# One kernel, one change: the first product of three blocks by 49 small products instead of 7 larger ones

## The chip, the cores and the metric

The kernel runs on one core of a Trainium2 chip. The core has five engines that run at the same time, each working through its own list of instructions in order: TensorE (PE, matrix products, with its weight loads shown as PEld), VectorE (DVE), ScalarE (ACT), GpSimd (POOL) and SyncE (SP), which here does nothing but issue DMAs. Data lies in HBM; on-chip memory of 128 partitions (SBUF) feeds the engines; TensorE writes into PSUM. The metric is the time of one execution in microseconds (us), the median of several runs.

## The reference

```python
# attention: q, k, v of shape (4, 8, 768, 64); gamma differs by head
for t in range(S):
    state = gamma * state + einsum('bhd,bhe->bhde', k[:, :, t], v[:, :, t])
    y[:, :, t] = scale * einsum('bhd,bhde->bhe', q[:, :, t], state)
x = y.transpose(0, 2, 1, 3).reshape(3072, 512)
h = x @ w_in                            # 512 -> 2048
g = h * (1 / (1 + exp(-1.702 * h)))
out = g @ w_out                         # 2048 -> 512
```

All of it is in float32 (the weights arrive as float64 and are narrowed in the kernel).

## The kernel before, in words

**Tiling.** The 3072 tokens are worked in `NB` = 6 blocks of 512, each of four attention chunks (a chunk is 64 tokens of two batch rows). A block's x lies transposed in the tile `X` as four quarters: two halves of the 512 features by two halves of the 512 tokens, each quarter two feature rows of 128 by 256 tokens. `X` has seven places, so that sums of quarters fit as well. `G` holds the gated hidden layer of one block, `W2` the weights of the second product, `W1A` and `W1B` those of the first (`W1B` in the two tiles tagged `late`, whose space is lent in between to `ring` and `own` of the second product, so that `W1B` is stored once and loaded again in each later block).

**Stages.** Block 0 uses plain products (`up0`), block 1 a form written out by hand (`seven`), blocks 2 to 5 `up(d)` for d = 0 to 3 (L555 to L597). A call of `up` computes a quarter of the hidden layer by the seven-product scheme: a 2 x 2 block product made of seven products of sums of quarters instead of eight. Each of the seven is four TensorE instructions of 128x128 weights against 256 columns (L562). ACT copies three partial results out of PSUM (L569, L576, L583), DVE adds PSUM and copy (L572, L580, L586, L588), ACT gates (L393), DVE forms sums for what follows (L594 to L597).

The second product of blocks 2 to 5 is `down49(m)`: two levels of the scheme, 49 products, each four instructions of 128 columns (L666), in 14 units (i, half), i from 0 to 6. Its inner weight sums were formed by `inner_w2` and lie in HBM (`W2D`); `stream` brings them back (POOL queue, L635), `derive` forms the sums of `G` (DVE, L655 to L657).

**Attention** is laid between units. After units 1, 4, 7 and 10 of `down49` of blocks 2 to 4 comes `step(j, j-1)`: PE computes `pa` and `py` (L289 to L312), DVE masks and adds, POOL scales k (`kd`, L274) and the state (L359). `step` reads q and k of its chunk transposed, which `turn(j)` does (DVE, L253). At its end, `turn(j)` issues the 16 loads of q and k for chunk j + 2 (SP, L157); `step(j)` issues four loads of k and four of v for chunk j + 1 (SP, L143). In `up` of block m, `turn` of the chunk that the first `step` of `down49(m)` needs stands after d = 0.

**Order.** On PE all instructions run as written. On the other engines a scheduler orders them, except those passed through `pin` or `keep_in_program_order`, which stay as written. SP's list is one: a DMA that waits holds all that are behind it.

Of the kernel before, what the change touches and what calls it, by code (L numbers as in the profile page):

```python
# [9 lines left out]
F32 = mybir.dt.float32  # L10
U32 = mybir.dt.uint32
AF = mybir.ActivationFunctionType
ALU = mybir.AluOpType
P = 128
# [14 lines left out]
def kernel(  # L29
# [59 lines left out]

    W1A = const.tile([P, NP // 2, 7, 2, P], F32, name="W1A")  # L90
    W1B = [late.tile([P, 2, 7, 2, P], F32, name=f"W1B{i}", tag=f"late{i}") for i in range(2)]
    W1D = [dram.tile([P, 2, 7, 2, P], F32, name=f"W1D{i}") for i in range(2)]
    W2D = [dram.tile([P, 3, NP // 2, P], F32, name=f"W2D{i}") for i in range(7)]
# [12 lines left out]
    whole_h = const.tile([P, H], F32, name="whole_h")  # L106
    ident = const.tile([P, P], F32, name="ident")
    mask = const.tile([P, 2, HP, D], F32, name="mask")
    state = [const.tile([P, 2, HP, D], F32, name=f"state{i}") for i in range(2)]


    def w1(p):

        return (W1A, p) if p < NP // 2 else (W1B[p // 2 - 2], p % 2)

# [66 lines left out]
    class Narrow:  # L182
# [4 lines left out]
        def __init__(self, i):  # L187
            n, p, h = (1 if i < 2 else 2), i // 2 % NP, i % 2

            if i < 2:  # L190
                m = W1A[:, 1, 2 * h:2 * h + 2].rearrange("p s c f -> p (s c f)")
                w = W1A[:, 0, h:4:2].rearrange("p ab c f -> p c ab f")
            elif i < NFF:
                t, q1 = w1(p)
                m = t[:, q1, 0:4].rearrange("p s c f -> p (s c f)")
                w = t[:, q1, 0:4].rearrange("p (ab h) c f -> p (h c) ab f", ab=2)
            else:
                m = w = W2[:, 0:4, p]
            x = raw(i, n).rearrange("p (n two) -> p n two", two=2)
            self.lo, self.hi, self.m, self.w, self.i = x[:, :, 0], x[:, :, 1], m, w, i  # L200
            if i >= NFF:
                self.lo, self.hi = [t.rearrange("p (s e) -> p s e", s=4) for t in (self.lo, self.hi)]
            self.mu = m.bitcast(U32)
# [191 lines left out]
    def g(m, p, s):  # L395

        if m:
            return G[:, p:p + 2, s, :]
        if s < 3:
            t, q1 = w1(p)  # L400
            return t[:, q1:q1 + 2, 4 + s].rearrange("p a c f -> p a (c f)")
        return X[:, 4 + p // 2] if p < 6 else G0
# [4 lines left out]
    def up0(th, p, tag):  # L407

        h = ps.tile([P, 2, TH], F32, name="ph", tag=tag)
        t, q1 = w1(p)  # L410
        for ab in range(2):
            for c in range(4):
                w = t[:, q1, 2 * ab + c // 2, c % 2, :]
                pe.matmul(h[:, ab], w, X[:, 2 * th + c // 2, c % 2, :], start=(ab == 0 and c == 0), stop=(c == 3),  # L414
                          skip_group_check=True)
        if th == 0:
            return t[:, q1, 4:6].rearrange("p s c f -> p (s c f)"), h
        return [(g1(0, p, 2 + i), i) for i in range(2)], h

    def up1(f):  # L420

        p, ab = divmod(f, 2)
        h = ps.tile([P, 2, TH], F32, name="ph", tag="xy"[f % 2])
        t, q1 = w1(p)
        for c in range(4):
            w = t[:, q1, 2 * ab + c // 2, c % 2, :]
            pe.matmul(h, w, X1[:, c // 2:4:2, c % 2, :], start=(c == 0), stop=(c == 3))
        return G[:, p, ab:4:2, :], h
# [12 lines left out]
    def seven_4(d):  # L441

        t, q1 = w1(2 * d)
        SUM_W[d] = m = [t[:, q1:q1 + 2, n].rearrange("p u c f -> p u (c f)") for n in range(4)]
        m.append(one.tile([P, 2, 2 * P], F32, name="w4", tag="qT", bufs=2))
        m.append(one.tile([P, 2, 2 * P], F32, name="w5", tag="at", bufs=2))
        m.append(two.tile([P, 2, 2 * P], F32, name="w6", tag="o"))
        pin(dve.tensor_add(m[4], m[2], m[3]))
# [72 lines left out]
    def sums_w1(p):  # L521
        t, q1 = w1(p)
        w = [t[:, q1:q1 + 2, s] for s in range(7)]
        pool.tensor_add(w[4], w[2], w[3])
        pool.tensor_sub(w[6], w[0], w[2])
        pool.tensor_sub(w[5], w[4], w[0])
        pool.tensor_sub(w[2], w[1], w[5])

    def sums_x():
        tc.keep_in_program_order(pool.tensor_sub(X[:, 4], X[:, 2], X[:, 0]))  # L530
        pool.tensor_sub(X[:, 6], X[:, 3], X[:, 2])
        pool.tensor_sub(X[:, 5], X[:, 3], X[:, 4])
        pool.tensor_sub(X[:, 2], X[:, 1], X[:, 5])

    def sums_w2(p):
# [19 lines left out]
    def up(d):  # L555

        t, q1 = w1(2 * d)

        def product(acc, sa, sb, start, stop):
            for u in range(2):  # L560
                for c in range(2):
                    pe.matmul(acc[:, u, :], t[:, q1 + u, sa, c, :], X[:, sb, c, :],  # L562
                              start=(start and u == 0 and c == 0), stop=(stop and c == 1), skip_group_check=True)
# [34 lines left out]


    ORDER = [(0, 0), (1, 2), (3, 5), (2, 6), (0, 4), (1, 3), (2, 1)]  # L600

# [29 lines left out]

    def stream(ring, i):

        c = ring[:, i % 2 * 3:i % 2 * 3 + 3]
        pool.dma_start(c, W2D[i])  # L635
        return c

    def begin_ring():

        ring = late.tile([P, 7, 4, P], F32, name="ring", tag="late0")  # L640
        return ring, {i: stream(ring, i) for i in range(2)}

    def down49(m, ring, comps):

        b, t0 = m * CB // NC * 2, m * CB % NC * D
        rows = out.rearrange("(b t) (e c) -> e t b c", b=B, c=EH)[:, t0:t0 + TH, b:b + 2, :] \
            .rearrange("e (h p) b c -> h e p b c", p=P)
        own = late.tile([P, 7, 4, P], F32, name="own", tag="late1")
        acc, kept = {}, {}

        def derive(i):
            q = [G[:, u::2, ORDER[i][0], h * P:(h + 1) * P] for u in range(2) for h in range(2)]
            a11, s3, a12, s2 = q
            d = own[:, i % 2 * 3:i % 2 * 3 + 3]
            dve.tensor_add(d[:, 0], s2, a11)  # L655
# [16 lines left out]

        flat = X[:, 4:6].rearrange("p s c t -> p (s c t)")
        def keep(name, half):
            if half == 0:
                if name in "pt":
                    home2(name, flat[:, 0:4 * P], flat[:, 4 * P:7 * P])
                else:
                    home2(name, (own if name == "u" else ring)[:, 6].rearrange("p j e -> p (j e)"),
                          one.tile([P, 2 * EH], F32, name=name, tag="s2" if name == "u" else "s3"))  # L680
            return kept[name][half]
# [16 lines left out]
        def then(i, half, p0):  # L698
            if i == 0:
                act.activation(keep("p", half), p0, AF.Copy)  # L700
            elif i == 1:
                put(0, 0, half, p0, "p")
            elif i == 2:
                act.activation(keep("u", half), p0, AF.Copy)
            elif i == 3:
                act.activation(keep("v", half), p0, AF.Copy)
            elif i == 4:
                u = kept["u"][half]
                dve.tensor_add(keep("t", half), p0, u)
                put(1, 1, half, p0, "v")  # L710
            elif i == 5:
                put(0, 1, half, p0, "t")
            else:
                put(1, 0, half, p0, "v")
# [21 lines left out]
        for i in range(7):  # L736
            for half in range(2):
                def unit(i=i, half=half):
                    if half == 0:
                        if i == 0:  # L740
                            pairs[0] = derive(0)
                        x = "x" if i in (0, 2, 3) else "y"
                        if i != 2 and i != 3:
                            for n in range(2):
                                acc[x, n] = ps.tile([P, 4 - n, P], F32, name="pq", tag=x)
                    x = "x" if i in (0, 2, 3) else "y"
                    if i == 6 and half == 1 and m == NB - 1:
                        finish(acc[x, half], pairs[i][half])
                        return
                    products(acc[x, half], pairs[i][half], i not in (2, 3))  # L750
                    then(i, half, acc[x, half])
                    if half == 0 and i < 6:
                        pairs[i + 1] = derive(i + 1)
                    if half == 1:
                        if i + 2 < 7:
                            comps[i + 2] = stream(ring, i + 2)
                        if i in (0, 1, 3):
# [208 lines left out]
    for m in range(NB):  # L966
# [8 lines left out]
        elif 1 < m < NB - 1:  # L975
# [3 lines left out]
            if last == NCH - 1:  # L979
                between.append(lambda: step(None, NCH - 1))  # L980
        if m > 1:
            if m > 2:
                W1B[:] = [late.tile([P, 2, 7, 2, P], F32, name=f"W1B{i}", tag=f"late{i}") for i in range(2)]
                pool.dma_start(W1B[0], W1D[0])
            for d in range(NP // 2):
                up(d)
                if d == 0 and m > 2:
                    pool.dma_start(W1B[1], W1D[1])
                if d == 0 and m < NB - 1:
                    turn((m + 1) * CB + 1)  # L990
                if d == NP // 2 - 2:
                    ring = begin_ring()
                if m == 2 and d < 2:
                    tc.keep_in_program_order(sp.dma_start(W1D[d], W1B[d]))
                if m == 2:
                    for i in range(2 * d, min(7, 2 * d + 2)):
                        inner_w2_t3(i)
        for n, unit in enumerate(down(m) if m < 2 else down49(m, *ring)):
            unit()
# [8 lines left out]
            if between and (n in (2, 5, 11, 16, 21) if m == 1 else n % 3 == (1 if m else 2)):  # L1008
                between.pop(0)()
            if 0 < m < NB - 1 and n == (23 if m == 1 else 11):  # L1010
                sums_x()


# [44 lines left out]
```

## Time and profile before

| | |
|---|---|
| median of 3 runs | 662.12 us (660.49 to 664.74) |
| the profiled execution: span | 660.5 us (no other time is recorded for it; the fastest run is 660.49) |
| PE busy | 642.2 us, 97% |
| DVE, POOL, ACT busy | 453.9, 198.8, 159.0 us |
| stage `up` of blocks 2, 3, 4, 5 | from 261.5, 362.9, 464.7 and 564.8 us, each 48.35 us |
| `down49` of blocks 2, 3, 4, 5 | from 309.9, 411.2, 513.1 and 613.2 us |

The page of a profile gives busy times per engine, the span in 40 slices, the DMA queues, the chain of work that ended last, and groups of instructions. Times inside a line are start or sum in us and mean ns of one. One TensorE instruction in float32 is two records in the trace, so "x8" in a timeline is four instructions.

### The profile page before, as it was taken

Reading aid. Unit: us, or ns where it says so; the run is one execution under the profiler, and the core shown is the slowest. Engines: PE = TensorE matmul, PEld = TensorE weight load, DVE = VectorE, ACT = ScalarE, POOL = GpSimd, SP = SyncE. Lnnn points to the kernel's source line nnn. Section 1 sums busy time; section 2 is a strip of 40 time slices with the busy share of each in tenths; the row PEclk is TensorE's granted clock in tenths of the full one; section 3 lists DMA queues with packets and bytes.
Section 4 is the critical chain, followed back from the end, with each engine's and each line's share of the span. In section 5 each row is a group of like instructions: output and inputs, shape, how many; then the busy total and the mean of one; then the engine's idle time right before and its main releaser. Section 6 shows DMA issues by size and latency. Waiting matters only on the chain.

```text
span 660.5 us, 15291 instructions
## 1 busy us (share of the span) xinstructions
PE 642.2 (97%) x6390; PEld 580.2 (88%) x6390; DVE 453.9 (69%) x645; ACT 159.0 (24%) x306; POOL 198.8 (30%) x225
## 2 busy tenths in 40 slices
PE   6789999999999999999999999999999999999997
PEld 3778888888788888889999888999888999988997
DVE  3699989999936973556984445995354995254965
ACT  4674233551000000333100233010233110233110
POOL 6400311310379217000536400445600255500000
PEclk9989999999999999999999999999999999999999
DMA  9995549763233556262485832386742252602142
GB/s 176 193 274 173 152 104 241 172 163 60 49 82 135 137 149 153 58 248 96 118 199 134 279 57 97 86 223 135 225 118 97 66 154 104 235 21 96 55 154 96
DMA packets 148149, 91.86 MB, mean 139 GB/s; under 512 B 131600, under 2 KB 134416, under 8 KB 147056
## 3 DMA queue, kind: packets, MB, share of 16 engines
q1 hardware_dynamic: 135856, 45.19, 29.8%
q0 software_dynamic: 9888, 44.46, 20.6%
q10 hardware_dynamic: 2336, 1.25, 0.6%
q8 instruction: 50, 0.82, 0.5%
q14 instruction: 19, 0.16, 0.1%
HBM read 72.89 MB, written 15.47 MB: 134 GB/s over the span
## 4 chain that ended last, share of the span: by engine, by line
PE 89%; DVE 4%; DMA 4%; SPq 1%; issue 1%; ACT 0%; DVEq 0%
PE pq L666 27%; PE px L562 17%; PE pd L799 13%; PE py L562 13%; PE ph L491 7%; PE ph L414 5%; PE pa L289 2%; PE py L312 2%; PE pa L297 2%; PE py L306 2%; DMA W<-in_moe_w_in_dram 1%; DMA W<-in_moe_w_out_dram 1%; DMA q_in<-in_q_dram 1%; PE pt L250 1%; SPq L140 1%
## 5 line engine op out<-in xcount | busy, mean ns | idle before, releaser
L635 POOL DMA_DIRECT2D ring<-W2D x28 | 15.4, 551 | 227.7 <-PE px L562 118.3
L666 PE MATMUL pq<-W,G 128*128 128x128 f32 x672 | 80.2, 276 | 0.0
L666 PEld LDWEIGHTS pq<-W,G 128*128 128x128 f32 x672 | 77.6, 192 | 1.3 <-issue 0.7
L666 PE MATMUL pq<-ring,own 128*128 128x128 f32 x448 | 60.1, 276 | 1.3 <-issue 1.3
L562 PE MATMUL px<-X,W1A 128*128 128x256 f32 x256 | 59.8, 379 | 0.0
L562 PE MATMUL px<-X,W1B 128*128 128x256 f32 x256 | 59.8, 379 | 0.0
L666 PEld LDWEIGHTS pq<-ring,own 128*128 128x128 f32 x448 | 54.5, 192 | 0.4
L562 PEld LDWEIGHTS px<-X,W1B 128*128 128x128 f32 x256 | 48.5, 190 | 6.7
L562 PEld LDWEIGHTS px<-X,W1A 128*128 128x128 f32 x256 | 48.4, 190 | 6.5
L393 ACT ACTIVATE G<-G 128x512 f32<-128x512 f32 x60 | 37.4, 628 | 54.7 <-DVE G L572 33.4
L799 PE MATMUL pd<-W,G 128*128 128x256 f32 x224 | 49.6, 381 | 0.0
L799 PEld LDWEIGHTS pd<-W,G 128*128 128x128 f32 x224 | 42.2, 190 | 5.9
L562 PE MATMUL py<-X,W1A 128*128 128x256 f32 x192 | 45.4, 379 | 0.0
L562 PE MATMUL py<-X,W1B 128*128 128x256 f32 x192 | 45.4, 379 | 0.0
L562 PEld LDWEIGHTS py<-X,W1A 128*128 128x128 f32 x192 | 36.5, 190 | 5.0
L562 PEld LDWEIGHTS py<-X,W1B 128*128 128x128 f32 x192 | 36.5, 190 | 5.0
L580 DVE TENSOR_TENSOR t<-py,u 128x512 f32<-128x512 f32 x16 | 11.1, 692 | 32.3 <-PE py L562 32.3
L569 ACT ACTIVATE p<-px 128x512 f32<-128x512 f32 x16 | 9.6, 597 | 96.0 <-PE px L562 96.0
L414 PE MATMUL ph<-X,W1A 128*128 128x256 f32 x128 | 30.6, 397 | 0.9 <-DVE X L347 0.9
L594 DVE TENSOR_TENSOR G<-G 128x512 f32<-128x512 f32 (+2 forms) x24 | 12.3, 513 | 25.7 <-ACT G L393 25.7
L666 PE MATMUL pq<-ring,G 128*128 128x128 f32 x224 | 29.6, 275 | 0.0
L666 PE MATMUL pq<-W,own 128*128 128x128 f32 x224 | 29.6, 275 | 0.0
(237 smaller groups left out, 1226.0 us busy)
## 6 DMA issues: line engine op xcount, KB each, us to landing
ring<-W2D POOLq DMA_DIRECT2D x28, 768.0 KB, 4.8
W1B<-W1D POOLq DMA_DIRECT2D x6, 1792.0 KB, 9.8
W<-in_moe_w_in_dram SPq DMA_DIRECT2D x12, 512.0 KB, 5.9
W<-in_moe_w_out_dram SPq DMA_DIRECT2D x10, 512.0 KB, 5.8
out_dram<-o POOLq DMA_DIRECT2D x20, 256.0 KB, 3.0
q_sq<-in_q_dram SPq DMA_DIRECT2D x144, 32.0 KB, 2.1
k_sq<-in_k_dram SPq DMA_DIRECT2D x144, 32.0 KB, 2.1
v_in<-in_v_dram SPq DMA_DIRECT2D x72, 64.0 KB, 3.1
```

The costliest lines, as they stand in the source:

```text
L289: pe.matmul(pa[HALF[w], u, 0, s, :], kt[HALF[u], w, s, :], qt[HALF[u], w, s, :], start=True, stop=True)
L297: pe.matmul(pa[HALF[u], w, 1, s, :], kd[HALF[w], HP * u + s, :], vn[HALF[w], HP * u + s, :], start=True, stop=True)
L306: pe.matmul(py[HALF[o], u, 1, 2 * w + s2, :], old[HALF[u], w, 2 * s2 + o, :], qt[HALF[u], w, 2 * s2 + o, :], start=True, stop=True)
L312: pe.matmul(py[HALF[o], w, 0, 2 * u + s2 if f < NEW else 2 * s2 + u, :], vn[HALF[w], HP * u + s, :], a[HALF[w], u, s, :], start=True, stop ...
L393: pin(act.activation(g, h[:, i], AF.Gelu_apprx_sigmoid))
L414: pe.matmul(h[:, ab], w, X[:, 2 * th + c // 2, c % 2, :], start=(ab == 0 and c == 0), stop=(c == 3), skip_group_check=True)
L491: pe.matmul(acc[:, u, :], w, x, start=(start and u == 0 and c == 0), stop=(stop and c == 1), skip_group_check=True)
L562: pe.matmul(acc[:, u, :], t[:, q1 + u, sa, c, :], X[:, sb, c, :], start=(start and u == 0 and c == 0), stop=(stop and c == 1), skip_group_ ...
L594: dve.tensor_sub(q[0][1], q[0][0], q[0][1])
L635: pool.dma_start(c, W2D[i])
L666: pe.matmul(p0[:, j, :], a[:, d], w[:, d], start=(new and j == 0 and d == 0), stop=(d == NP // 2 - 1), skip_group_check=True)
L799: pe.matmul(p0[:, n, :], g1(m, p, sa)[:, n * P:(n + 1) * P], W2[:, sb, p, :], start=(new and p == 0 and n == 0), stop=(last and p == NP - ...
```

## The change

Blocks 3 to 5 compute the first product by `up49` in place of `up`. Each of the seven products is itself made of seven products of 128 x 128 x 128, so a block has 4 x 49 = 196 instructions of 128 columns in place of 112 of 256. The units (a product P1 to P7 of a pair d) are written in an order that interleaves the four pairs; the attention's PSUM buffers (`pa`, `py`) are used for the odd pairs. A unit has two halves, of four and three instructions. The seven inner results are combined by five adds for each quarter (`post`, on POOL or DVE as the table `then` says), before the gate.

The inner sums of x are formed in place and by `derive_x` (DVE); those of the weights once, in block 2 (`inner_w1`: DVE, POOL, stored to HBM as `T1D` and `Q1D` by SP), and come back in every block of 3 to 5 by 28 loads on SP (`fetch_t` of 192 or 384 KB, `fetch_q` of 256 KB). Five of them are issued after unit 11 of `down49` of the block before (`before_up49`), the others within `up49`. `w_in` is laid out as `W1A` (the four quarters) and `W1L`, a view of the tile `LATE` (the three sums); in blocks 3 to 5 `LATE` holds what is fetched, the sums of x, and the working space of `down49`. `turn` of the chunk that the first `step` of `down49` needs stands behind `up49` as a whole; the first two `stream`s of each of these blocks go to SP. In `down49` one kept partial result (`t`) goes, as its products are added in PSUM.

```diff
-    W1A = const.tile([P, NP // 2, 7, 2, P], F32, name="W1A")
-    W1B = [late.tile([P, 2, 7, 2, P], F32, name=f"W1B{i}", tag=f"late{i}") for i in range(2)]
-    W1D = [dram.tile([P, 2, 7, 2, P], F32, name=f"W1D{i}") for i in range(2)]
+    W1A = const.tile([P, NP, 4, 2, P], F32, name="W1A")
+    LATE = late.tile([P, 2 * NP * 3, P], F32, name="LATE")
+    W1L = LATE.rearrange("p (n s c) f -> p n s c f", s=3, c=2)
+    T1D = [dram.tile([P, 7, 3, P], F32, name=f"T1D{d}") for d in range(NP // 2)]
+    Q1D = [dram.tile([P, 2, 3, 2, P], F32, name=f"Q1D{d}") for d in range(NP // 2)]
...
+    def sums_x_inner():
+        lo, hi = [slice(i * P, (i + 1) * P) for i in range(2)]
+        x = X[:, 0:4]
+        pin(dve.tensor_sub(x[:, :, 0, hi], x[:, :, 0, lo], x[:, :, 0, hi]))
+        pin(dve.tensor_sub(x[:, :, 1, hi], x[:, :, 1, hi], x[:, :, 0, hi]))
+        sums_x()
+        derive_x(0)
...
+    def inner_w1(d):
+        b11, b12, b21, b22 = w1_quarters(d, 0)
+        t = []
+        for k, a in enumerate((b12, b22, b21)):
+            t.append(one.tile([P, 4, P], F32, name=f"w1t{k}", tag="at", bufs=2) if k != 1 else
+                     two.tile([P, 4, P], F32, name=f"w1t{k}", tag="tmp", bufs=1))
+            tc.keep_in_program_order(dve.tensor_sub(t[k], a, t[k - 1] if k else b11))
+            sp.dma_start(T1D[d][:, 0:4, k], t[k])
...
+    UNITS = [("P1", 0), ("P2", 0), ("P1", 1), ("P2", 1), ("P6", 0), ("P5", 0), ("P7", 0), ("P4", 0), ("P3", 0),
+             ("P6", 1), ("P5", 1), ("P7", 1), ("P1", 2), ("P4", 1), ("P2", 2), ("P3", 1), ("P6", 2), ("P5", 2),
+             ("P7", 2), ("P1", 3), ("P4", 2), ("P2", 3), ("P3", 2), ("P6", 3), ("P5", 3), ("P7", 3), ("P4", 3),
+             ("P3", 3)]
...
+    def fetch_t(d, s, slot):
+        n = 1 if s == 6 else 2
+        c = LATE[:, SLOT[slot]:SLOT[slot] + 3 * n].rearrange("p (s k) f -> p s k f", k=3)
+        pin(sp.dma_start(c, T1D[d][:, s:s + n]))
...
+    def before_up49():
+        fetch_t(0, 0, "C")
+        fetch_t(1, 0, "B")
+        for s in (5, 4, 6):
+            fetch_q(0, s)
...
+        def products(p0, prod, d, half):
...
+            pairs = [(a12, b21), (s2, t2), (s3, t3), (d0, t1)] if half == 0 else [(a11, b11), (d2, t4), (d1, b22)]
+            new = prod in ("P1", "P2", "P5")
+            for j in ((0, 2, 1, 3) if half == 0 else (0, 2, 1)):
+                a, b = pairs[j]
+                pe.matmul(p0[:, j, :], b, a, start=(new and j == 0), stop=True, skip_group_check=True)
...
+        def post(eng, d, s):
...
+            pin(eng.tensor_add(top, top, m1))
+            pin(eng.tensor_add(h1u0, h1u0, h0u1))
+            pin(eng.tensor_add(one_e(2), one_e(2), h1u1))
+            pin(eng.tensor_add(h1u1, h1u1, h1u0))
+            both = at(b + 1, d, [*K, [7 * P, 2]])
+            pin(eng.tensor_add(both, both, E[:, :, 1:3] if K else E[:, k, 1:3]))
...
+        A, B = (0, 3), (1, 2)
+        then = {
+            1: [lambda: derive_x(1), lambda: fetch_t(0, 2, "C")],
...
+            15: [lambda: fetch_t(2, 2, "C"), lambda: post(dve, 1, B), lambda: presum(0, B), lambda: outer(0)],
+            16: [lambda: fetch_q(3, 5), lambda: gate(1, A)],
+            17: [lambda: fetch_q(3, 4), lambda: fetch_t(3, 4, "B")],
+            18: [lambda: fetch_q(3, 6), lambda: fetch_t(3, 6, "S"), lambda: post(pool, 2, A), lambda: gate(1, B),
+                 lambda: presum(1, A)],
+            21: [lambda: post(dve, 3, (0,))],
+            22: [lambda: fetch_t(3, 2, "C"), first_stream, lambda: post(pool, 2, B), lambda: presum(1, B), lambda: outer(1)],
+            23: [lambda: gate(3, (0,)), lambda: gate(2, A)],
+            24: [lambda: presum(3, (0,)), lambda: presum(2, A)],
+            25: [lambda: post(dve, 3, (3,))],
+            26: [lambda: post(pool, 3, (1,)), lambda: gate(3, (3,)), lambda: gate(2, B)],
+            27: [lambda: post(dve, 3, (2,)), lambda: gate(3, (1,)), lambda: gate(3, (2,)), lambda: presum(2, B),
+                 lambda: outer(2), lambda: presum(3, (3,)), lambda: presum(3, (1,)), lambda: presum(3, (2,)),
+                 lambda: outer(3)],
+        }
...
+                if prod in ("P1", "P6", "P7"):
...
+                    pin(act.activation(kept[name][half], p0, AF.Copy))
+                elif prod == "P4":
+                    pin(act.activation(place(d, 1, half), out(p0, half), AF.Copy))
+            if prod == "P2":
+                add(d, 0, "p", "y")
+            elif prod == "P7":
+                add(d, 3, "v", "y")
+            elif prod == "P3":
+                add(d, 2, "u", "y")
...
-        if m > 1:
-            if m > 2:
-                W1B[:] = [late.tile([P, 2, 7, 2, P], F32, name=f"W1B{i}", tag=f"late{i}") for i in range(2)]
-                pool.dma_start(W1B[0], W1D[0])
...
+        elif m > 2:
+            comps = {}
+            ordered[0] = True
+            up49(first_stream=lambda: comps.update({0: stream(0, sp)}))
+            ordered[0] = False
+            if m < NB - 1:
+                turn((m + 1) * CB + 1)
+            comps[1] = stream(1, sp)
...
+            if 1 < m < NB - 1 and n == 11:
+                ordered[0] = True
+                sums_x_inner()
+                before_up49()
+                ordered[0] = False
```

## The prediction

> **What bounds the kernel now.** I read the page's busy times first, then the windows of each stage, then the chain of work that ended last.
>
> ```profile
> PE 642.2 (97%) x6390; PEld 580.2 (88%) x6390; DVE 453.9 (69%) x645; ACT 159.0 (24%) x306; POOL 198.8 (30%) x225
> ```
>
> ```profile
> 362.80:411.20 48.40, 48.40 (x227) 42.61 (x226) 21.90 (x34) 16.40 (x27) 9.52 (x13) 1.00 0.49 148
> 411.20:464.70 53.50, 52.85 (x906) 52.02 (x905) 42.65 (x64) 3.87 (x7) 25.84 (x29) 1.00 0.57 140
> ```
>
> The columns of the windows are length and sum, then PE, PEld, DVE, ACT, POOL, clock, DMA share, GB/s. PE works without a gap in block 3's `up` (48.4 us) and nearly so in its `down49`. So time goes only if PE has less to do, and comes back wherever PE must wait. DVE is idle for more than half of `up`, but for only a fifth of `down49`.
>
> **What PE saves.** The chain gives the rate of 128-column instructions:
>
> ```profile
> 411.22 6.25 PE pq L666 x56
> 613.16 43.78 PE pq L666 x392
> ```
>
> 392 records are 196 instructions: 0.2233 us each. A block's `up` is 112 instructions in 48.35 us, `up49` 196 in 43.8. Three blocks: 3 x 4.6 = **-13.9 us**, if PE never waits.
>
> **First wait: SP's list at the start of blocks 3 and 4.** The timeline of SP in block 2's `down49` and after (start, length, count):
>
> ```profile
> 319.95 3.48 SPq L143 DMA_DIRECT2D kn_in<-in_k_dram  x4
> ...
> 358.48 4.01 SPq L157 DMA_DIRECT2D q_sq<-in_q_dram  x8
> 362.60 3.90 SPq L157 DMA_DIRECT2D k_sq<-in_k_dram  x8
> 366.59 2.58 SPq L143 DMA_DIRECT2D kn_in<-in_k_dram  x4
> 369.27 2.79 SPq L143 DMA_DIRECT2D v_in<-in_v_dram  x4
> 379.14 5.95 SPq L157 DMA_DIRECT2D q_sq<-in_q_dram  x8
> ```
>
> From 319.95 to 372.06 SP issues 80 loads without a rest, 0.65 us each. Waits cannot explain it; SP's waits in that stretch are
>
> ```profile
> SPq L143 <- POOL kd L274: 32.3, 1, 32.3
> ...
> SPq L157 <- DVE qT L253: 0.5, 1, 0.5
> ```
>
> the first of which is the one before 319.95. So SP finishes this list 9.2 us after `up` of block 3 has begun (362.87). Today that is harmless. In the compiled order of the changed kernel the same 80 loads stand there, released by the same `kd`, and behind them the five fetches of `before_up49`. The first (384 KB) is issued at 372.1 and lands some 3.5 us later (an estimate between 256 KB stores, 3.0 us, and 768 KB `ring` loads, 4.8 us, in the page's DMA list). P1 of pair 0 needs it in its third instruction, at 363.3. **+12.5 us** (bounds 10 and 15). The later fetches follow at about 0.65 us, the units at 1.56, so they keep ahead.
>
> **Second wait: the transposes that moved.** `turn` stood after d = 0 of `up`; now it is behind `up49`, and on DVE behind its whole tail. From the last unit's release to the second transpose DVE has, by the rows for each width (512 elements 0.69, 384 0.55, 256 0.42, 128 0.29, 1024 1.21): rest of `add` and `derive(0)` 1.9, `post`, `add`, `post` 4.7, `presum` of pairs 2 and 3 and `outer` of both 5.3, `sums_g_outer` 1.2, `derive(1)` 2.1, transposes 1.4: 16.6 us, of which 1.6 lie under the last unit. PE comes to `step` after units 0 and 1, 28 instructions or 6.25 us. 15.0 - 6.25 = 8.8; independent DVE instructions start 0.60 apart instead of 0.69, which takes up to 2.2. I take 8 in blocks 3 and 4 (bounds 5 and 10): **+16**. Block 5 has no `step`, but its second product (slot 1) needs `presum` and `derive(1)` from the same tail: **+2** (0 to 4).
>
> **Third: SP again, block 4.** In block 3's `down49` the 16 loads that `turn` issues also move: they wait for the transposes, end of `up49` + 15 us, and 96 loads follow at 0.65 = 62.5, so the first fetch lands at 15 + 62.5 + 4 = 81.5. PE is there after 53.5 + 8 + 0.5 = 62. **+18.5** (at the fastest row, 8 in 4.00 us, only +5). In block 4 there are 28 loads, and the fetches are early: nothing.
>
> **Fourth: DVE and POOL within `up49`.** DVE had 21.9 us of work in `up`. Now: 12 `add` pairs of 1.24, `derive_x` 2.9, four `post` 7.8, `presum` 7.3, `outer` 5.5, `derive(0)` 2.1, 40 us in 43.8. POOL gets five `post` of pairs (2 x 1.27 + 3 x 0.75 = 4.8 each) and a single of 2.8, 27 us. Both read two SBUF inputs, and the trace shows what happens when they meet: `inner_w2`'s subtractions alone, then beside POOL's sums:
>
> ```profile
> 249.01 1.42 DVE L612 TENSOR_TENSOR X<-W,X 128x512 f32<-128x512 f32 x2
> 200.49 4.09 DVE L612 TENSOR_TENSOR X<-W,X 128x512 f32<-128x512 f32 x2
> ```
>
> ```profile
> 201.07 1.28 POOL L526 TENSOR_TENSOR W1A<-W1A 128x512 f32<-128x512 f32 x1
> ```
>
> 0.7 us becomes 2.0: one waits for the other. (Additions that read PSUM keep their 0.68 beside POOL.) The tight place is the end. From P3 of pair 1 (25.0 us into the stage) DVE is free at 26.4 and has 17.4 us of listed work until the `add` that frees P3 of pair 3's PSUM, due at 42.1: 1.7 late by its own work. Two POOL `post`s of pair 2 lie in the same stretch, 9.5 us; some 4 of them can hide under the `add`s from PSUM. 1.7 + 9.5 - 4 = 7.2; I take 7 in each block, **+21** (bounds 1 and 11 each).
>
> **Small terms.** Block 2: 16 DVE and 16 POOL instructions and 36 stores (`inner_w1`) beside a DVE that is half idle; the stores of one shared buffer follow each other through SP and reach into the last quarter: +0.5 (0 to 4). PE after a long wait: at 21.8 us of the trace, when PE had mostly waited, four transposes' eight records took twice their later time, and at 26 us still did:
>
> ```profile
> 21.81 1.11 PE L250 MATMUL pt<-ident,kn_in 128*128 128x128 f32 x4
> 31.65 0.60 PE L250 MATMUL pt<-ident,kn_in 128*128 128x128 f32 x4
> ```
>
> Before, PE never waits long after that; now four times by 8 us or more. PE was slow for 5.5 us without rest from 20.75, which loses up to 2.3 us. I take 1 for each: **+4** (0 to 9). [...]
>
> [...]
>
> **Sum.** -13.9 + 12.5 + 16 + 2 + 18.5 + 21 + 0.5 + 4 = +60.6 on the profiled span of 660.5: 721. The median of the runs lies 1.6 above that span: **723 us**.
>
> **Rivals.** (a) DVE and POOL don't hinder each other in `up49` (other tiles, other order of arrival): 21 becomes 3, **705**. For it: collisions in the trace don't always lengthen DVE. (b) SP gets through its list in time, as 32 KB loads may go faster than when DMAs of `W1B` and stores compete (their bytes are gone from the POOL queue): no first and third wait, two restarts fewer, 60.6 - 31 - 2 = 27.6, **690**. Against it: the waits listed above are too short to be the pace. (a) and (b) together **672**. (c) On the other side, faster: all loads, transposes and DVE's tail hide, and only PE counts: 660.5 - 13.9 + 1 for copies that end just late (P7 to P4) + 1.6: **649**. It decides if SP's fetches land before 363.3 and the transposes end within 6.25 us of `up49`. Only a different order of instructions than the compiled one would do it. (d) The products themselves don't run at 0.223, as each goes to another PSUM place instead of four in a row: at the 276 ns of one such matmul, +10.4 a block, of which 7 hide under DVE's lag: **733**.
>
> **Chances.** Forecast 0.56 (710 to 740), (a) 0.17, (b) 0.09, both 0.05, (c) 0.05, (d) 0.05; no change 0.03. The range of 8 in 10 runs from 685, near (b), to 745, which takes in (d) and the upper bounds of two terms. Faster by over 1% (about what this kernel's runs can tell from no change) 0.05, within 1% 0.03, slower 0.92.
>
> **What would show it.** Right: PE idle at the first unit of blocks 3 and 4, put to a DMA of `LATE`; PE `pa` waiting for DVE `qT` once in blocks 3 and 4; SP's list unbroken over both stage borders; block 5 the shortest of the three; DVE lines of `post` above 0.8 us for 256 elements. Wrong: SP idle before the fetches, or `up49` at 44 us in all blocks.

## The result, and the profile after

The changed kernel takes **755.7 us** (median of 4 runs, 754.1 to 758.7) against 663.4 us (660.5 to 665.0) of the kernel before on the same chip: 1.140 times as long, 95% interval 1.135 to 1.144. The forecast was 723, with a range of 685 to 745: the sign was right, the size 33 us short. The profiled execution has a span of 754.9 us, 94.4 more than before.

The page's line of busy times and its row of the granted clock:

```profile
PE 653.8 (87%) x6894; PEld 602.8 (80%) x6894; DVE 533.9 (71%) x794; ACT 182.1 (24%) x348; POOL 300.9 (40%) x319
...
PEclk9999999999999999999779998995999899999999
```

PE's share has fallen from 97% to 87%, and its clock now dips, which it never did before after the start. DVE has 80 us more to do, POOL 102. The windows of the first and second product of block 3, and of the first product of block 5 (length and sum, PE, PEld, DVE, ACT, POOL, clock, DMA share, GB/s):

```profile
364.57:444.64 80.07, 52.66 (x394) 50.63 (x393) 36.66 (x63) 21.98 (x38) 35.51 (x37) 0.85 0.48 138
444.64:505.90 61.26, 54.99 (x906) 53.96 (x905) 49.91 (x80) 5.99 (x10) 27.40 (x34) 0.94 0.58 142
...
644.79:707.50 62.71, 50.17 (x394) 47.91 (x393) 38.34 (x65) 22.08 (x38) 32.08 (x34) 0.95 0.42 130
```

Before, these were 48.40, 53.50 and 48.30 us. Even block 5, which has no late fetch and no late transposes, takes 14.4 us longer, and the clock falls to 0.85 in block 3. What PE waited for (total, times, longest):

```profile
PE pw L707 <- DMA LATE<-T1D: 31.2, 2, 15.7
PE pw L707 <- ACT u L819: 18.1, 6, 3.3
PE pa L295 <- DVE kT L259: 12.5, 2, 6.2
PE pw L707 <- ACT p L819: 6.2, 6, 1.2
PE pw L707 <- ACT v L819: 4.5, 6, 0.7
PE pw L707 <- ACT G L821: 4.2, 6, 0.8
```

The first and third line are the forecast's fetches and transposes. The others (34.9 us, with 1.9 for `v49b` further down) are waits for **ACT's copies out of PSUM**, for which the forecast's sum has nothing (its rival (c) allows 1 us for copies from P7 to P4). Those shown come 6 times each: twice a block, for pairs 1 and 3. Pairs 0 and 2 run the same code and have none. The difference is in `banks`: an even pair's accumulator is two PSUM tiles, one for each half of a unit; an odd pair's is one tile of 8 places, cut in two. In the compiled order PE's second half of an odd pair carries a wait for ACT's copy of the first half, although it writes other places.

The chain of work that ended last shows what stands before such a copy, in block 5, from DVE's `add` after P7 of pair 0 on (its short pieces named `issue` are left out):

```profile
659.17 0.47 DVE e L736
659.73 1.27 POOL G L754
661.07 0.73 POOL G L755
661.79 0.70 POOL e L756
662.56 0.73 POOL G L757
663.36 1.27 POOL G L759
664.65 0.04 ACT e L821
665.04 0.60 ACT u L819
665.68 5.04 PE pw L707 x28
```

POOL's `post` of pair 0 takes 4.9 us. The buffer `e49` has two places; P4's copy on ACT needs the one that this `post` is reading, so it waits; the copy of `u` stands behind it on ACT; and PE's second half of P6 stands behind that copy. In pair 3 the way is longer: DVE's add for P2 waits for POOL's `post` of pair 2, DVE's own `post` and the first add that reads `u` of pair 2 follow it, and only then may ACT write the next `u` (timeline):

```profile
692.29 0.56 DVE L736 TENSOR_TENSOR e<-pw,LATE 128x384 f32<-128x384 f32 x1 [1.08 <-POOL G L759]
...
695.34 0.60 ACT L819 ACTIVATE u<-pw 128x512 f32<-128x512 f32 x1 [5.90 <-DVE G L736]
```

What PE does after the wait for `u` of pair 1 (timeline; x2 is one instruction):

```profile
662.46 0.39 PE L707 MATMUL pw<-LATE 128*128 128x128 f32 x2
665.68 0.49 PE L707 MATMUL pw<-X,w1q 128*128 128x128 f32 x2 [2.84 <-ACT u L819]
666.01 0.39 PE L707 MATMUL pw<-LATE,w1q 128*128 128x128 f32 x2
...
667.17 0.63 PE L707 MATMUL pw<-X,LATE 128*128 128x128 f32 x2
...
670.09 0.39 PE L707 MATMUL pw<-X,LATE 128*128 128x128 f32 x2
```

From 666.5 to 670.1 instructions start 0.43 us apart instead of 0.22. Summed over the stretches in which they do, PE lost 9.5 us after the six waits for u, 5.2 after the two fetches and 3.5 after the two waits for kT: **18.2 us**.

With these, the span's 94.4 us add up:

| | forecast | measured |
|---|---|---|
| PE's saving | -13.9 | -13.7 |
| waits for fetches (terms 1 and 3) | 12.5 + 18.5 | 31.2 |
| transposes, block 5's tail (term 2) | 16 + 2 | 12.5 + 0 |
| waits within `up49` (term 4) | 21 | 35.3 |
| slow clock after waits | 4 | 18.2 |
| blocks 0 to 2 | 0.5 | 1.8 |
| ends of waits | none | 9.1 |

The last row is the remainder, and has a size of its own: idle time is counted from a record's end, 0.39 us after its start, where the next instruction would have started after 0.22, and the one after a wait lasts 0.1 longer. That is some 0.28 us for each of 32 waits, 9.0.

### The profile page after: what moved, and what is told of

It reads as the page before. It is cut to its first block, busy times and chain, and to the rows that moved or that the text cites. A ratio compares the mean times of both kernels' runs of the same rounds, so it can differ in the third digit from the quotient of the medians.

```text
span 754.9 us, 16847 instructions
## 1 busy us (share of the span) xinstructions
PE 653.8 (87%) x6894; PEld 602.8 (80%) x6894; DVE 533.9 (71%) x794; ACT 182.1 (24%) x348; POOL 300.9 (40%) x319
## 4 chain that ended last, share of the span: by engine, by line
PE 60%; DVE 16%; POOL 8%; DMA 7%; SPq 3%; issue 3%; ACT 2%; DVEq 0%; ACTq 0%; POOLq 0%
PE pq L893 20%; PE pd L1025 13%; PE pw L707 8%; PE ph L493 6%; PE ph L418 4%; PE pa L295 2%; DVE e L736 2%; POOL G L754 2%; POOL G L759 2%; DMA G<-in_moe_w_in_dram 1%; DVE G L769 1%; PE px L613 1%; PE py L318 1%; PE py L312 1%; SPq L150 1%
## 5 line engine op out<-in xcount | busy, mean ns | idle before, releaser
L707 PE MATMUL pw<-LATE 128*128 128x128 f32 x336 | 70.2, 293 | 0.4 <-DVE LATE L554 0.4
L707 PE MATMUL pw<-X,W1A 128*128 128x128 f32 x288 | 51.9, 291 | 12.7 <-ACT p L819 6.2
L707 PE MATMUL pw<-X,LATE 128*128 128x128 f32 x168 | 35.7, 297 | 31.2 <-DMA LATE<-T1D 31.2
L707 PE MATMUL pw<-X,w1q 128*128 128x128 f32 x216 | 41.8, 308 | 22.6 <-ACT u L819 18.1
L893 PE MATMUL pq<-LATE 128*128 128x128 f32 x448 | 59.8, 276 | 0.0
L707 PEld LDWEIGHTS pw<-LATE 128*128 128x128 f32 x336 | 56.3, 210 | 0.6 <-DVE LATE L554 0.6
L418 PEld LDWEIGHTS ph<-X,W1A 128*128 128x128 f32 x256 | 49.1, 194 | 8.2 <-DVE X L353 1.1
L707 PEld LDWEIGHTS pw<-X,W1A 128*128 128x128 f32 x288 | 42.0, 201 | 16.2 <-ACT p L819 7.3
L893 PEld LDWEIGHTS pq<-LATE 128*128 128x128 f32 x448 | 54.5, 192 | 0.4
L1025 PE MATMUL pd<-W,LATE 128*128 128x256 f32 x160 | 35.1, 380 | 0.0
```

The source lines that it names most:

```text
L707: pe.matmul(p0[:, j, :], b, a, start=(new and j == 0), stop=True, skip_group_check=True)
L893: pe.matmul(p0[:, j, :], a[:, d], w[:, d], start=(new and j == 0 and d == 0), stop=(d == NP // 2 - 1), skip_group_check=True)
L1025: pe.matmul(p0[:, n, :], g1(m, p, sa)[:, n * P:(n + 1) * P], W2[:, sb, p, :], start=(new and p == 0 and n == 0), stop=(last and p == NP - ...
```

## The experiments

The times of the edits are of one execution each, unless an interval is given. The time at which block 3 begins varied between 361.3 and 369.5 us among these runs, without an edit that touches PE's work before it; so I compare the lengths of stages and the time from block 3's beginning to the end ("rest"), beside the whole time.

| | time | first product of blocks 3, 4, 5 | second, 3 and 4 | rest |
|---|---|---|---|---|
| before | 659.4 to 665.0 | 48.4, 48.4, 48.4 | 53.5, 51.7 | 297.8 |
| changed | 755.7 | 80.1, 79.0, 62.7 | 61.3, 59.9 | 390.3 |
| e1 late copies | 739.3 | 73.6, 72.6, 55.8 | 63.2, 62.5 | 376.1 |
| e2 early transposes | 744.5 | 76.6, 76.9, 62.5 | 55.9, 53.8 | 373.1 |
| e3 loads behind fetches | 728.2 | 65.6, 66.8, 62.7 | 60.8, 61.3 | 364.5 |
| e4 without POOL's `post` | 733.6 | 73.1, 72.5, 56.5 | 60.7, 59.6 | 369.8 |
| e5 = e1 and e4 | 713.9 | 64.3, 63.8, 47.0 | 62.6, 61.1 | 346.1 |
| e6 = e1, e2 and e3 | 708.1 | 60.0, 55.7, 55.9 | 62.0, 60.2 | 342.3 |
| e7 PE kept busy | 751.4 | 77.5, 77.0, 62.7 | 60.4, 61.3 | 386.3 |
| e8 = e1 without `post(2, B)` | 731.8 | 72.6, 69.9, 52.9 | 62.3, 60.3 | 365.7 |
| e9 = e1 without `post(2, A)` | 730.3 | 70.8, 69.5, 52.0 | 62.6, 61.5 | 364.8 |
| e10 = e6 without POOL's `post` | 675.6 | 49.0, 46.2, 47.0 | 62.8, 57.7 | 310.1 |
| e11 = e6 without any `post` | 671.7 | 48.3, 47.1, 46.6 | 59.7, 53.3 | 302.4 |

**e1: copies after both halves.** In an odd pair PE writes both halves before ACT copies either.

```diff
-                    pin(act.activation(kept[name][half], p0, AF.Copy))
+                    copies.append((kept[name][half], p0))
...
-                    pin(act.activation(place(d, 1, half), out(p0, half), AF.Copy))
+                    copies.append((place(d, 1, half), out(p0, half)))
+                if d % 2 == 0 or half == 1:
+                    while copies:
+                        pin(act.activation(*copies.pop(0), AF.Copy))
```

> The copies of an odd pair's halves (P1, P6, P7, P4) are issued after both halves' products. Theory 'one tile': the two halves of an odd pair's accumulator are one PSUM tile, so PE's second half waits for ACT's copy of the first; of the 34.9 us that PE waits for ACT in the changed kernel some 23 go (what stays is before P7 and P4, 4 us a block), with the refill after each wait (0.3 us, 30 times, two thirds of them) and most of the slow stretches after the 3 us waits (1.6 us, 6 times): 718 us (710 to 728). Theory 'DVE and POOL hinder each other' (the prediction's fourth term): DVE stays as late as it was, and PE waits for it at the next product instead: 745 to 757.

Measured 739.3: between the two. PE's waits for p, v and G are gone, which shows that they came from copies that stood between the two halves; that it is the shared tile which ties the second half to them is read from `banks`, the compiled order and the even pairs, as two tiles for an odd pair were not tried. For u 1.9 us are left, for `v49b` 3.4. And new waits stand in the place of the others (waits of PE in e1):

```profile
PE pw L707 <- ACT UB L825: 7.8, 6, 1.6
PE pw L707 <- issue: 6.0, 3, 2.0
PE pw L707 <- DVE e L736: 5.1, 2, 2.5
```

So neither theory has the whole: with the tile's waits gone, a lag of DVE and ACT that they had covered comes out: block 5's first product, which waits for no fetch, is still 12 us over PE's 43.8.

**e2: the two transposes of `turn` after unit 26,** ahead of DVE's tail; the 16 loads that `turn` issues follow the second `stream`.

```diff
-            26: [lambda: post(pool, 3, (1,)), lambda: gate(3, (3,)), lambda: gate(2, B)],
+            26: [lambda: post(pool, 3, (1,)), lambda: gate(3, (3,)), lambda: gate(2, B), early],
...
-            if m < NB - 1:
-                turn((m + 1) * CB + 1)
             comps[1] = stream(1, sp)
+            while LATER:
+                load(*LATER.pop(0))
```

> The two transposes of turn stand within the first product, after unit 26, instead of behind it; the 16 loads that turn issues follow the second stream. If the prediction's second term is right, the two waits of PE for kT (6.2 us each) go, with a slow stretch of 1.7 us after each, and block 4's fetches come earlier, since their list on SP starts some 11 us sooner: 755 - 12.5 - 3.5 - 4 = 735 us (729 to 741). If DVE's tail is only handed on, PE waits for derive(1) or for mask instead: 745 to 752.

The whole time (744.5) misses the range, but here block 3 began 4.9 us later than in the changed kernel. From there on it saves 17.2, against 20 expected: the waits for kT are gone but for 0.3 us, the second products are 5.4 and 6.1 us shorter, and the fetches were waited for 27.4 us instead of 31.2. PE waits for nothing of `derive(1)` in the second products; new there are 2.2 us for DVE's `o`, 1.9 of them in block 3.

**e3: the last 24 attention loads of SP's list behind the fetches.**

```diff
-        if 2 * CB <= j < NCH - 2:
+        if j in (4 * CB, 5 * CB):
+            LATER.append((j + 2, "qk"))
+        elif 2 * CB <= j < NCH - 2:
             load(j + 2, "qk")
...
-        if j is not None and 2 * CB < j < NCH - 1:
+        if j in (4 * CB, 5 * CB):
+            LATER.insert(0, (j + 1, "v"))
+        elif j is not None and 2 * CB < j < NCH - 1:
             load(j + 1, "v")
```

> The last 24 attention loads of SP's list in blocks 2 and 3 (8 of k and v, 16 of q and k) are issued behind the fetches, within and after the first product. If the prediction's first and third terms are right (SP's list), the two waits for T1D fall from 15.6 to 0 to 3 us each, with the slow clock after them (2.3 us each): 755 - 28 - 4.5 = 722 us (717 to 732). If the fetches are late for another reason (their own time, or the slots they wait for), the waits stay over 8 us: 740 to 755.

728.2, inside the range. This line of PE's waits in e3 is all that is left of 31.2 us:

```profile
PE pw L711 <- DMA LATE<-T1D: 4.4, 2, 3.4
```

Terms 1 and 3 stand: the fetches were late because of what stood before them on SP. From block 3's beginning on the run saves 25.8 us, somewhat less than the waits and their slow stretches, as a wait of 3.6 us for the copy p in block 3 and a slow stretch after it are new.

**e4: without POOL's `post`** (an early return for `eng is pool`; six of the table's ten calls, not of eight).

> The changed kernel without the combining adds that POOL does (six of the eight `post` calls of pairs 0 to 3 that the table gives to POOL are left out, so the gated values are not those of the reference). Theory 'one tile': the waits for ACT's p, v, G and v49b (16.8 us) stay, since they come from the tile; those for u fall from 18.1 to about 5, since only there ACT stands behind a POOL `post`; and the slow stretches after u (9.5 us) go: 733 us (728 to 740). Theory 'DVE and POOL hinder each other' alone: all 35 us go, with their slow stretches: 703 us (698 to 712).

733.6, as the first theory has it. PE's waits in e4:

```profile
PE pw L707 <- ACT u L821: 8.4, 6, 2.3
PE pw L707 <- ACT p L821: 6.4, 6, 1.5
```

Only u fell (to 8.4, where 5 was expected: in pair 1 the waits are 0.7 each, in pair 3 still 1.9 to 2.3); p, v (4.5) and G (4.2) stayed; and with no wait over 2.3 us left in `up49` but the fetches, no slow stretch follows any of them.

**e5: both edits together.**

> The late copies of odd pairs (739 us) and POOL's `post` calls left out as well. If what was left in the first product after the first edit (12 us a block over PE's 43.8) comes from POOL, by the length of its `post` or by hindering DVE, block 5's first product takes 46 to 47.5 us instead of 55.8 and the run 714 us (709 to 720). If DVE's own list is what is late, it stays over 52 us, and the run at 730 or more.

713.9, and block 5's first product takes 46.95 us: 3.2 over PE's work, and less than `up` took. So all but 3 of the 19 us that block 5's `up49` loses are the tile and POOL. Alone the edits save 6.9 (e1) and 6.3 us (e4) there, together 15.8: each of the two had hidden part of the other.

**e8 and e9: which way POOL costs.** Both are e1 less one call, `post(pool, 2, B)` or `post(pool, 2, A)`.

> The late copies of odd pairs (739 us) without one call, POOL's `post` of pair 2, quarters 1 and 2. If it hinders DVE, DVE's presum and outer instructions beside it take 0.4 and 0.7 us instead of 1.38 and 1.1, PE's wait for DVE's e before the last unit (2.5 us in blocks 4 and 5) goes, and the 2.0 us wait before P5 of pair 3 stays: 733 us (730 to 736). If DVE's own list makes that wait, it stays: 738 to 740.

> The late copies of odd pairs (739 us) without one other call, POOL's `post` of pair 2, quarters 0 and 3, whose `e49` buffer the second half of P2 of pair 3 takes. If its length (5 us on POOL) holds up DVE's add there, PE's wait before P5 of pair 3 (2.0 us in each block) goes, and most of the one for ACT's copy that follows (1.6 us), while the wait for DVE before the last unit (2.5 us in blocks 4 and 5) may stay: 739 - 3 x 3.5 = 728 us (724 to 733). If DVE is late there by its own list, the waits stay: 737 to 740.

731.8 and 730.3. In e8 PE's wait for DVE's e is gone, and the one before P5 stayed (6.0 in 3); in e9 it is the other way round (7.6 in 3 for DVE's e, none before P5). So both ways are real. Each edit takes out a whole call, its length and its hindrance together; which of the two acts is read from the wait that goes. Hindrance, on DVE in e1 beside POOL's `post`, and then the same two DVE instructions in e8:

```profile
679.17 0.42 DVE L768 TENSOR_TENSOR G<-G 128x256 f32<-128x256 f32 x1
679.40 1.31 POOL L754 TENSOR_TENSOR G<-G,e 128x512 f32<-128x512 f32 x1 [3.57 <-DVE e L736]
679.62 1.37 DVE L769 TENSOR_TENSOR G<-G 128x256 f32<-128x256 f32 x1
```

```profile
675.28 0.42 DVE L768 TENSOR_TENSOR G<-G 128x256 f32<-128x256 f32 x1
675.73 0.42 DVE L769 TENSOR_TENSOR G<-G 128x256 f32<-128x256 f32 x1
```

The call is worth 2.95 us in block 5 (55.80 to 52.85), here where the tile's waits are gone; with them in place PE has no wait for DVE's e, and the same call was not taken out alone. The other call, which acts by its length on POOL through the two places of `e49`, is worth 3.8 (55.80 to 52.00).

**e7: PE kept busy during the fetch waits.**

```diff
+                if (prod, d, half, j) == ("P1", 0, 0, 1) and warm:
+                    t = ps_a.tile([P, 8, P], F32, name="warm", tag="pa")
+                    for i in range(warm):
+                        pe.matmul(t[:, i % 2 * 4:i % 2 * 4 + 4], ident, ident[:, None, :].to_broadcast([P, 4, P]),
+                                  start=True, stop=True)
```

> The changed kernel with 17 products of 512 columns (14.6 us at full speed) that PE does for nothing while it waits for the fetch at the head of blocks 3 and 4. If PE's slow stretches come from having been idle, the 5.2 us lost after these two waits go and the rest stays: 750 us (748 to 752). If PE is slow there for what it reads, nothing changes: 754 to 757.

751.4. In both blocks PE starts at full pace after the fetch (instructions 0.22 us apart), and the 5.2 us are gone; the slow stretches after u, whose waits the edit leaves alone, are there after five of the six (1.4 to 1.75 us each), while after the wait of 3.13 us in block 4 there is none. It is idleness that makes PE slow, but not its length alone; the last section shows what decides.

**e6: the three edits together,** timed in two runs: 1.070 times the kernel before, interval 1.060 to 1.080.

> The three edits together. If the three causes add: 755 - 37 - 16 - 33 = 669 us (660 to 682), about the kernel before. If 'DVE and POOL hinder each other' holds, DVE's lag stays in each block: 690 to 710.

The result lies in the rival's range. The fetches (3.1 us are left, in block 3) and the tile are out of the way, but the first products stay at 55.7 to 60.0 us, by POOL as e5 and e10 show, and the second products of blocks 3 and 4 at 60 to 62. There DVE has most of its tail to do; these are e6's window of block 3's second product, whose DVE column was 42.65 before, and 20 us of it in which DVE has no gap:

```profile
425.97:488.00 62.03, 55.22 (x907) 53.67 (x906) 53.20 (x82) 5.88 (x10) 28.05 (x34) 0.97 0.67 158
...
445.00:465.00 20.00, 16.95 (x369) 16.48 (x368) 20.00 (x27) 2.18 (x4) 8.55 (x9) 1.00 0.73 189
```

**e10 and e11: what would be left.** e6 without POOL's `post`, and e6 without any (an unconditional return).

> The three edits together (708 us), and POOL's `post` calls left out: what remains when every wait found so far is gone. The first products fall as in the run with late copies and without those calls, by 9 us each: 708 - 27 = 681 us (675 to 687). So even without a part of its work the changed kernel would be slower than the kernel before, because of DVE's tail in the second products of blocks 3 and 4 (8 us each), block 2 (3 us) and the rest. If these calls are also what delays that tail, 665 or less.

> The three edits together, and no `post` call at all, on POOL or DVE (the values are not those of the reference). DVE has 7.8 us less in each block, most of it in the tail: if DVE's amount of work is what delays PE in the second products of blocks 3 and 4, these take 55 to 57 us instead of 61, and the run 668 us (661 to 675). If they are late for another reason, 678 or more.

675.6 and 671.7. Without POOL's part the first products of blocks 4 and 5 take 46.2 and 47.0 us, 2.2 and 1.4 less than before: the gain that PE's fewer instructions leave. The second products of blocks 3 and 4 are still 9.3 and 6.0 us longer than before, and without DVE's `post` 6.1 and 1.6 longer: DVE's amount of work is a large part of it. In block 3 POOL's `kd`, whose loads the third edit delays, is 2.5 us of the rest; what makes up the remainder was not separated. Since even a kernel that leaves out its combining adds is slower than the one before (one execution of it, 671.7 against 659.4 to 665.0), I take it that no other share of these calls between DVE and POOL would bring the change under it; none was tried.

## Why the prediction was wrong

**PE's saving** was right: the instructions run at the row's 0.2233 us, and rival (d) has nothing for it.

**First and third wait (SP's list)**: right in the mechanism; 31.2 against 31 together, singly 15.7 and 15.5 instead of 12.5 and 18.5. The first lies outside its bounds (10 to 15), and that the sum comes out so close is luck: the two errors cancel. This is the beginning and the end of SP's list over block 3's border (timeline of SP):

```profile
324.68 2.58 SPq L150 DMA_DIRECT2D kn_in<-in_k_dram  x4
...
376.76 1.08 SPq L664 DMA_DIRECT2D LATE<-T1D  x2
```

80 loads in 52.0 us, 0.65 each, as in the trace before; the fetch landed after 4.1 us. The list began 2.8 us later in its stage than I had put it. In block 4 the list began 11.9 us behind `up49` instead of 15, and 96 loads took 61.5 us, 0.64 each. Rival (b) is out.

**Second wait (transposes)**: right in its place, and e2 shows it; 6.2 each instead of 8, and block 5's 2 us were hidden. The forecast named qT; PE waits for kT, the second of the pair.

**Fourth (within `up49`): the step that failed.** It put 7 us a block down to DVE and POOL hindering each other. The hindrance exists, but mostly in `presum` and `outer` (1.38 us for 256 elements instead of 0.42, 1.10 for 512 instead of 0.69); of DVE's `post` only the last of a block has a line above 0.8 us (0.94 or 0.95 for 256 elements), so that this sign of the forecast's last part held once a block. In the changed kernel none of PE's waits within `up49` but 0.4 us is for DVE, so what the hindrance costs lies under other waits. What PE waited for instead were the copies out of PSUM, through two places that I had not checked: the single PSUM tile of the odd pairs, and the two places of `e49`, which put POOL's 4.9 us ahead of PE. I had looked for PSUM being freed by DVE's `add`, not for what ACT's copies free. Size: 11.8 us of waiting a block instead of 7, and 3 us of ends of waits. Rival (a), no hindrance, would have lowered the forecast; the truth lay on the other side.

**Slow clock: the term that was mis-sized most in proportion.** 18.2 instead of 4, by count and by price. I counted four long waits; there were ten, since the six of 2.8 to 3.3 us were followed by slow stretches as well. And I took 1 us for each, where the rows give some 1.6 after u, 1.6 to 1.9 after kT and 2.3 to 2.9 after a fetch. Waits of 2.84 us were enough here, and by the last section 1.95 us are, if they fall into one stretch of the clock.

**Block 2**: its two products take 3.0 us longer (51.6 and 52.8 us against 48.4 and 53.0), within the bounds (0 to 4); blocks 0 and 1 ended 1.2 us sooner, which leaves the table's 1.8. The other signs held: block 5's first product is the shortest of the three, and SP's list runs over both borders without a rest.

## What to carry to other kernels

Where PE is 97% busy, fewer PE instructions are worth their time only if every other engine's list fits under the shorter stage: compare busy time with stage length, stage by stage (DVE went from 21.9 us in 48.4 to 37 with PE's own 43.8), before counting the saving. For every partial result in PSUM ask which tile it is in, who copies it, and what stands ahead of that copy on its engine; here the second of two halves in one tile waited for the copy of the first (6.2 us in all for `p`). Count waits as well as their sum: most of those of about 3 us cost half as much again in PE's pace (the six for `u` 18.1 us, and 9.5 after them).

## What the runs showed of the hardware

A DVE subtraction of 128 x 256 from SBUF takes 0.42 us alone (in e8) and 1.37 (in e1) beside POOL's add of 1.31 that began 0.22 us before it: DVE's ends 0.28 us after POOL's has.

A wait of about 3 us mostly slows PE, but not always: of the 24 waits for u of 2.8 to 3.3 us in the changed kernel, e2, e3 and e7, 21 were followed by a slow stretch and three by none. What decides can be read from the traces. In each trace the granted clock changes only at instants that lie whole multiples of 3.413 us apart, wherever the waits are. Counted over these stretches of 3.41 us, from 45 us to PE's last instruction and over all 13 traces, the full clock was halved after each of the 71 in which PE was idle for 1.95 us or more, and after none in which it was idle for 1.94 us or less (in the changed kernel after ten, of 2.05 to 3.41 us, and after none of 1.88 or less). Two windows of the changed kernel around a wait of 2.84 us, and three of e7 around the wait of 3.13 us, which falls into two stretches, show it (length, PE's busy time, and the clock, third from the end):

```profile
400.35:403.77 3.42, 1.23 (x11) 1.24 (x12) 0.56 (x1) 1.19 (x3) 2.61 (x3) 1.00 0.25 96
403.77:407.18 3.41, 3.41 (x19) 3.41 (x18) 0.00 (x0) 0.28 (x1) 3.18 (x4) 0.50 0.28 80
```

```profile
562.31:565.72 3.41, 1.88 (x17) 1.69 (x16) 2.18 (x7) 0.00 (x0) 1.26 (x1) 1.00 0.11 36
565.72:569.14 3.42, 1.82 (x16) 1.82 (x17) 3.35 (x6) 1.40 (x3) 1.90 (x2) 1.00 0.82 313
569.14:572.55 3.41, 2.51 (x21) 2.12 (x19) 3.34 (x4) 1.81 (x4) 3.25 (x4) 1.00 0.00 1
```

In the first, PE idles 2.19 us of a stretch, and the next runs at half clock, which costs at most half of its 3.41, 1.7 us; in the second 1.53 and 1.60, and nothing follows. Several short waits can add up in the same way. In e1 the same three waits (1.99, then 1.4 to 1.6, then 1.13 us, all within 10 us) were followed by slow stretches of 1.4 and 1.9 us in block 3, where one stretch held 1.95 us of idle time, and by none in blocks 4 and 5, where none held over 1.62. In e4 waits of 2.3 and 1.9 us had none. Where the stretches begin differs from trace to trace (a stretch at half clock begins at 36.96 us in the kernel before and at 38.54 in the changed one, 1.58 apart where one is 3.41 long), so a forecast can give such a wait only a chance of costing.
